# State space scan and SiLU layer on one core: signs of eleven weight blocks on ScalarE, three more W_in blocks in one-pass products, a new order of the ramp

## The chip, the cores and the metric

The kernel runs on one core of one Trainium2 chip. The core has five engines that run side by side and in order, each through its own queue: TensorE (PE, matrix products; PEld is its loading of the stationary operand), VectorE (DVE), ScalarE (ACT), GpSimd (POOL) and SyncE (SP, which here only issues DMA transfers). The metric is the time of one execution on the device, in microseconds (us); lower is better. Before the change the median of three runs is 329.29 us (328.35 to 331.6). A profiled execution of the same kernel was recorded by the hardware profiler, and all views quoted are views of such a record.

## The reference

The first stage is a state space scan (Mamba-2, SSD): for 4 batches and 8 heads over 768 positions, in chunks, with state size 16 and head size 32.

```python
# per batch and head, chunk c, positions i and j in it
cum = cumsum(log(a)); L = exp(cum_i - cum_j) for i >= j
y = (C B^T * L) x + exp(cum_i) * C state          # inside the chunk, and from the state
state = exp(sum log a) * state + sum_j exp(cum_last - cum_j) B_j x_j
```

Its output, turned to 3072 tokens of 256 features, goes through a layer with SiLU, with W_in of 256 x 2048 and W_out of 2048 x 256:

```python
h = x @ w_in
g = h * (1.0 / (1.0 + np.exp(-h)))
return (g @ w_out).astype(np.float32)
```

The weights arrive as 64-bit floats; everything else, and the result, is fp32.

## The kernel before, in words

**Units and groups.** The 3072 tokens are cut into twelve units of 256 tokens (u = 0 to 11, three to a batch), and into six groups of 512 tokens (G = 0 to 5, two units each). For each unit PE does the scan in four bursts of small products: `ab` (decay rows are transposed; units 0 and 1 alone), `g0` (C against B, line 585), `gd` or `D` (B against x, line 571) and `Y` (lines 635 and 644). DVE does the running products `E` (line 512), the masks `M` (line 600) and the state `S` (line 615). ACT moves results out of the accumulators: `X0` (line 666, units 0 and 1) and `y` (line 672), `SM` (line 623), `ce` (line 546), `b` (line 594), `tq` (line 540). For units from 2 on, decays are prepared once for all (`ir` loads, `AA`, `AP`, `AD`), written to a scratch in memory and loaded back (`La`, `Lp`).

**Weight blocks.** W_in is cut into eight blocks of 256 columns (n = 0 to 7) and W_out into eight blocks (n = 8 to 15). A block is loaded raw (`lw,n`, 512 KB, line 288) as pairs of 32-bit words of the 64-bit number, and made into fp32 without arithmetic in 64 bits, over 128 x 512 elements at a time: `u` (ACT, line 294) takes the size of the high word, `v` (ACT, line 297) turns the top bits of the low word into mantissa bits, `w,n,0` and `w,n,1` (DVE, lines 303 and 307) clamp the high word and shift it by three, `w,n,2` (DVE, line 310) puts the sign bit of the high word into v, and `W` (POOL, line 318) adds u and v as integers. Two of the 16 blocks take `W` in two halves.

**Two ways to multiply.** In fp32 a product of 128x512 takes two recorded passes. For most of the work the operands are therefore split into three parts whose products run in one pass each: `H` (ACT, line 322) makes the high part of a weight block, `lD` (DVE, line 326) or `Wl` with `Wm` the low part, `dD` (DVE, line 330) or `Wd` with `We` the third. For the tokens the same three parts are made by `xh` (line 679) and `x,u,0` and `x,u,1` (lines 651 and 654). The first layer is then `a,G,i` (high and low parts, eight products of 128x512 into accumulators ga or gb, line 800), `ax` (ACT, a rescaling in place, line 811), `d` (third part, four products) and `dg` (ACT, SiLU, line 821). The second layer is `q` (line 782) on the parts `h`, `l` and `e` (lines 827, 651 and 837) of the SiLU result.

**Group 0 is done otherwise**, since PE needs work while weights still arrive: W_in blocks 0 to 5 are multiplied in fp32 (`s,u,j`, line 697, for each of the units 0 and 1, into one of three accumulators hp), with `si` (ACT, SiLU, line 703); blocks 6 and 7 go through `a`, `ax`, `d`, `dg`. Its second layer is in fp32: `n1,f,m` (line 761), two accumulators of hp for the whole length.

**What sets the order.** Every instruction stands in a list written out by hand or by a planner beforehand, the string SCHEDULE: its 1309 words are executed from left to right when the program is made, so each engine's queue has its instructions in that order; a second table, SLOTS, says which buffer each tile takes. There is no run-time choice: an engine waits at the head of its queue until the tiles of that instruction are there. The words `z` are products of zeros that keep PE running before it has work (line 441). "The ramp" is here the part up to the point at which the lists of before and after become the same, early in group 1. Loads are issued by SP, except where a word's last number is 1 (ACT's queue) or where POOL issues them (`AD`, `Wm`, `We`).

Of the kernel before, what the change touches and what calls it, by code (L numbers as in the profile page):

```python
# [8 lines left out]
FP32 = mybir.dt.float32  # L9
# [18 lines left out]
Ln,2,0,1,0 xh,1 W,12 x,1,0 w,8,1 v,13 w,13,2 W,13 lw,15 u,15 w,8,2 Ln,2,1,1,0 si,1,5 s,1,4 a,0,7 si,1,4 n1,9,0 H,12  # L28
Wd,12 x,0,1 lw,14 u,14 n1,11,0 n1,9,1 x,1,1 W,8 Ln,2,1,0,0 v,14 w,14,2 ir,0 si,1,0 n1,1,0 n1,1,1 H,0 n1,0,1 H,1 lw,6 v,6
w,6,2 n1,11,1 n1,10,1 ir,2 ir,1 u,6 lw,10 Wl,12 AA,0 AA,1 AD,4 w,6,0 AP w,6,1 AD,0 lw,2 Ln,2,0,0,0 ax,0,7 w,15,0 u,10  # L30
u,2 W,6 n1,8,0 AD,1 v,2 H,6 v,10 w,2,0 s,1,1 si,1,1 lw,3 tp,2 dD,7 v,3 v,15 u,3 w,2,1 w,2,2 W,2,0 Lt,3,1,3,0 lD,6 dD,6
w,14,0 n1,8,1 w,3,2 a,0,6 ax,0,6 w,15,2 W,2,1 s,1,2 si,1,2 H,2 d,0,7 w,14,1 dg,0,7 AD,2 w,3,0 w,15,1 d,0,6 dg,0,6 W,14
Lt,3,1,0,0 w,10,2 s,0,2 lw,9 u,9 v,9 Lt,3,1,2,0 Lt,3,1,1,0 T,3,1 H,4 si,0,2 n1,10,0 Lx,2,0,0 n1,12,1 La,2,0,0 w,3,1 tq,2
# [24 lines left out]
d,2,3 q,2,1,0,0 Lt,7,0,3,0 Vd,1,1 Ln,8,0,0,0 ax,2,2 d,2,2 e,2,0 q,2,0,1,1 q,2,0,0,0 dg,2,3 dg,2,2 Lx,7,0,0 Lt,7,0,1,0
Lt,7,0,2,0 T,7,0 h,2,3 l,2,3 g0,7 gd,7 b,7,0 Lt,8,0,2,0 q,2,0,1,0 q,2,1,1,1 M,7,1 e,2,3 q,2,0,0,1 o,1,0,2 q,2,1,0,1
Lt,8,1,3,0 a,2,5 q,2,3,1,1 Lp,7,0 b,7,1 o,1,1,2 O,1,1,2,2,0 S,7,0 S,7,1 ax,2,5 S,7,2 O,1,0,2,3,0 Lx,8,0,0 M,7,0  # L60
q,2,3,1,0 h,2,2 SM,7,0 S,7,3 O,0,0,2,2,0 La,8,0,0 Lt,8,0,0,0 a,2,4 l,2,2 SM,7,1 ax,2,4 Lt,8,1,0,0 d,2,5 dg,2,5 h,2,5
# [827 lines left out]
```

## Time and profile before

| what | before |
|---|---|
| median of 3 runs | 329.29 us (328.35 to 331.6) |
| the profiled execution: its time, its span | 329.13 us, 327.4 us |
| busy in the span: PE, DVE, ACT, POOL | 319.7, 240.9, 209.6, 55.2 us |
| granted TensorE clock, mean | 0.996 |

The span is from the first to the last recorded instruction; 1.73 us of the execution lie outside it. Busy time is the time in which an engine has at least one instruction under way; matmuls overlap, and their ends are modelled, so a busy PE still may have small holes. The chain view follows the work that ended last back from the end, from each instruction to what released it. A row of the window view gives a stretch's length, and then each engine's busy time in it with the number of instructions. A row of the group view reads: line, engine, operation, tile written and tiles read, shape, count | busy time, mean ns of one | idle time of the engine just before. A row of the timeline reads: start, duration, engine, line, operation, tiles, shape, count, and in brackets the idle time before it with what ended it.

### The profile page before, as it was taken

What the parts mean: (1) busy time and instruction counts of PE and PEld (TensorE: products, weight loads), DVE (VectorE), ACT (ScalarE), POOL (GpSimd) and SP (SyncE); (2) the same over time, 40 slices, a digit from 0 to 9 for tenths busy, and PEclk for the clock granted to TensorE, in tenths of its full rate; (3) what the DMA queues carried; (4) which work ended last, traced back from release to release, by engine and by line L of the source; (5) the groups of instructions that cost most, each with busy time, mean ns of one, the idle gap of its engine ahead of it and who ended that gap; (6) DMA issues with size and microseconds to landing.
All of it is one profiled execution on the core that took longest, in us unless ns stands there. A gap on an engine that the chain in (4) does not pass through costs nothing.

```text
span 327.4 us, 7522 instructions
## 1 busy us (share of the span) xinstructions
PE 319.7 (98%) x3067; PEld 243.1 (74%) x3067; DVE 240.9 (74%) x331; ACT 209.6 (64%) x319; POOL 55.2 (17%) x74
## 2 busy tenths in 40 slices
PE   8889999999999999999999999999999999999994
PEld 4568576655687778878887778878887788888883
DVE  5898999999988966877688199665787544635553
ACT  4679878648696846584761874837775355674641
POOL 1364766316102330000200010010001000000000
PEclk9999999999999999999999999999999999999998
DMA  6999955367872663423632306514042000050002
GB/s 163 208 287 291 271 137 144 52 145 133 149 132 46 104 117 50 90 33 66 143 80 62 51 1 110 110 26 97 3 72 38 9 2 2 0 88 0 2 1 64
DMA packets 94962, 29.27 MB, mean 89 GB/s; under 512 B 80000, under 2 KB 86912, under 8 KB 94928
## 3 DMA queue, kind: packets, MB, share of 16 engines
q1 hardware_dynamic: 90960, 25.71, 36.1%
q0 software_dynamic: 1616, 2.82, 4.9%
q10 hardware_dynamic: 2352, 0.26, 0.6%
q8 instruction: 24, 0.39, 0.5%
q14 instruction: 10, 0.08, 0.1%
HBM read 22.81 MB, written 3.34 MB: 80 GB/s over the span
## 4 chain that ended last, share of the span: by engine, by line
PE 93%; SPq 3%; DMA 2%; issue 0%; DVE 0%; DVEq 0%
PE hp L782 29%; PE ga L800 18%; PE gb L800 18%; PE hp L761 9%; PE hp L697 6%; PE o_ps L782 6%; DMA s2k<-in_B_dram 2%; PE ga L585 2%; PE ga L635 2%; PE ga L644 2%; PE ga L571 1%; PE gb L644 1%; SPq L269 1%; SPq L262 1%; SPq L288 1%; SPq L375 0%
## 5 line engine op out<-in xcount | busy, mean ns | idle before, releaser
L782 PE MATMUL hp<-r4k,s2k 128*128 128x512 f32 x400 | 110.0, 394 | 0.0
L651 DVE SCALAR_TENSOR_TENSOR r4k<-r4k,r4k 128x1024 fp32r<-128x1024 f32 (+1 forms) x42 | 50.4, 1201 | 51.0 <-ACT r4k L827 47.9
L782 PEld LDWEIGHTS hp<-r4k,s2k 128*128 128x128 f32 x400 | 74.0, 188 | 16.4 <-issue 0.3
L800 PE MATMUL ga<-raw,s2k 128*128 128x512 f32 x240 | 62.3, 395 | 0.0
L800 PE MATMUL gb<-raw,s2k 128*128 128x512 f32 x240 | 61.1, 390 | 0.0
L800 PEld LDWEIGHTS ga<-raw,s2k 128*128 128x128 f32 x240 | 44.7, 188 | 11.4 <-ACT ga L811 0.9
L800 PEld LDWEIGHTS gb<-raw,s2k 128*128 128x128 f32 x240 | 44.8, 188 | 9.8 <-ACT gb L811 0.5
L837 DVE SCALAR_TENSOR_TENSOR r4k<-r4k,r4k 128x1024 fp32r<-128x1024 f32 x40 | 49.2, 1231 | 3.4 <-DVE r4k L651 0.9
L827 ACT ACTIVATE r4k<-r4k 128x1024 fp32r<-128x1024 f32 x40 | 42.2, 1058 | 3.2 <-issue 1.3
L811 ACT ACTIVATE ga<-ga 128x1024 f32<-128x1024 f32 x21 | 21.1, 1007 | 24.6 <-PE ga L800 23.8
L811 ACT ACTIVATE gb<-gb 128x1024 f32<-128x1024 f32 x21 | 21.2, 1009 | 17.6 <-PE gb L800 13.3
L782 PE MATMUL o_ps<-r4k,s2k 128*128 128x512 f32 x80 | 30.7, 390 | 0.0
L761 PE MATMUL hp<-r4k,s2k 128*128 128x512 f32 x64 | 30.0, 602 | 0.0
L821 ACT ACTIVATE r4k<-gb 128x1024 f32<-128x1024 f32 x21 | 21.4, 1020 | 12.4 <-PE gb L800 9.9
L520 POOL TENSOR_TENSOR BT<-bn,ab 128x256 f32<-128x256 f32 x10 | 6.7, 671 | 129.2 <-DVE ab L512 129.2
L318 POOL TENSOR_TENSOR s2k<-s2k,s2k 128x512 uint32<-128x512 uint32 (+1 forms) x19 | 23.6, 1249 | 25.8 <-DVE s2k L310 12.7
L821 ACT ACTIVATE r4k<-ga 128x1024 f32<-128x1024 f32 x21 | 21.5, 1023 | 8.4 <-PE ga L800 8.2
L512 DVE TENSOR_TENSOR_SCAN ab<-ab,diag 128x512 f32<-128x512 f32 x20 | 24.8, 1264 | 0.0
L697 PE MATMUL hp<-r4k,s2k 128*128 128x256 f32 x96 | 22.2, 381 | 0.0
L697 PEld LDWEIGHTS hp<-r4k,s2k 128*128 128x128 f32 x96 | 18.0, 190 | 3.9 <-issue 1.4
L761 PEld LDWEIGHTS hp<-r4k,s2k 128*128 128x128 f32 x64 | 11.6, 189 | 10.5 <-issue 9.6
L782 PEld LDWEIGHTS o_ps<-r4k,s2k 128*128 128x128 f32 x80 | 15.0, 188 | 3.2
(123 smaller groups left out, 383.8 us busy)
## 6 DMA issues: line engine op xcount, KB each, us to landing
ab<-az SPq DMA_DIRECT2D x20, 256.0 KB, 4.2
raw<-in_moe_w_in_dram SPq DMA_DIRECT2D x8, 512.0 KB, 4.3
raw<-in_moe_w_out_dram SPq DMA_DIRECT2D x8, 512.0 KB, 6.7
out_dram<-r4k SPq DMA_DIRECT2D x44, 64.0 KB, 2.3
xt<-in_x_dram SPq DMA_DIRECT2D x20, 128.0 KB, 3.6
s2k<-s2k POOLq DMA_DIRECT2D x10, 256.0 KB, 4.0
pfx<-ac SPq DMA_DIRECT2D x10, 130.0 KB
bn<-in_B_dram SPq DMA_DIRECT2D x20, 64.0 KB, 4.6
```

The lines of the kernel that those rows point to most:

```text
L318: nc.gpsimd.tensor_tensor(out=u[:, :, fs], in0=u[:, :, fs], in1=v[:, :, fs], op=ALU.add)
L512: nc.vector.tensor_tensor_scan(out=o, data0=src, data1=diag.rearrange("p h t -> p (h t)"), initial=0.0, op0=ALU.mult, op1=ALU.add)
L644: nc.tensor.matmul(out=y[w][32 * q:32 * q + 32, c, 64 * k:64 * k + 64], lhsT=xc[64 * c:64 * c + 64, k, h], rhs=m[64 * c:64 * c + 64, k, h] ...
L651: nc.vector.scalar_tensor_tensor(out=l, in0=f32(h), scalar=BACK, in1=y, op0=ALU.mult, op1=ALU.add)
L697: nc.tensor.matmul(out=hp[:, i], lhsT=WT[j][:, kc, 128 * i:128 * i + 128], rhs=XM()[:, 2 * kc:2 * kc + 2, u], start=(kc == 0), stop=(kc == ...
L761: nc.tensor.matmul(out=NP[m], lhsT=WT[8 + f // 2][:, f % 2, 128 * m:128 * m + 128], rhs=GT[0, f // 2][:, f % 2], start=(n == 1), stop=(n = ...
L782: nc.tensor.matmul(out=ACC[P, c], lhsT=WK[8 + i, p][:, k, 128 * m:128 * m + 128], rhs={"h": HT, "l": LT, "d": DT}[p][P, i][:, k], start=(n ...
L800: nc.tensor.matmul(out=o, lhsT=WK[j, q][:, kc, 128 * i:128 * i + 128], rhs=xs[:, 2 * kc:2 * kc + 2], start=(start and q == "h" and kc == 0 ...
L811: nc.scalar.activation(t, t, AF.Copy, scale=1.0 + Z)
L821: nc.scalar.activation(g, t, AF.Silu, scale=BACK)
L827: nc.scalar.activation(t, GT[G, i], AF.Copy, scale=-LESS * Z)
L837: nc.vector.scalar_tensor_tensor(out=DT[G, i], in0=f32(HT[G, i]), scalar=-1.0, in1=f32(LT[G, i]), op0=ALU.mult, op1=ALU.subtract)
```

## The change: what it does

1. **Signs on ScalarE.** For blocks 0, 4, 5, 12, 13, 6, 2, 14, 10, 3 and 9 the word `w,n,2` on DVE goes, and a word `g,n` on ACT comes: an activation Sign of the high word, with a bias held in a tile (`above`, a column of one tiny value), that writes +1 or -1 as bf16 into the upper half of each word of v. So that these upper halves are right, `v` is made with half the scale, and all weights come out halved; the five other blocks (7, 1, 8, 11, 15) keep `w,n,2`. The factors of two are given back by scales that instructions have already.
2. **Three more one-pass blocks in group 0.** The six words `s` with their six `si` for blocks 1, 2 and 3 go; `a`, `ax`, `d` and `dg` for G = 0 and i = 1, 2 and 3 come. The parts of the weights that they need were made before too, for the later groups; they now are made earlier.
3. **A new order of the ramp.** The list has 1310 words, and its last 710 are the same as before. The ramp ahead of them is put in another order, loads included, and the table of buffers is new.

```diff
 SCHEDULE
...
-Ln,0,0,0,1 ia,1 ci z,1 z,1 z,1 z,1 z,1 z,1 ia,0 Ln,0,0,1,1 cI z,1 ch cP ct ip,0,0 z,1 z,1 z,1 c1 cd A AT cp AU lw,0 z,1
...
-S,0,3 Ln,1,1,0,0 ab,1,0 E,1,0 C,0 Y,0 X0,0,1 Ln,1,0,1,0 B,1,1 X0,0,0 u,5 w,5,0 ip,1,0 z,1 P01,1,0 tp,1 tq,1 s,0,0 ce,1,1
-ce,1,0 g0,1 Lx,1,1,0 Lx,1,0,0 W,4 xh,0 w,5,1 si,0,0 B,1,0 P01,1,1 D,1 s,0,4 M,1,1 lw,1 u,1 lw,12 S,1,0 W,5 v,1 ca S,1,1
-S,1,2 SM,1,0 SM,1,1 lw,13 s,0,5 si,0,5 v,12 C,1 M,1,0 Y,1 w,1,0 w,1,1 W,7 si,0,4 lw,8 w,1,2 W,1,0 z,1 w,12,2 X0,1,0 H,7
-S,1,3 X0,1,1 x,0,0 lD,7 u,12 w,12,0 w,12,1 u,13 w,13,0 w,13,1 W,1,1 s,0,1 u,8 v,8 s,1,5 ir,3 w,8,0 si,0,1 s,1,0 co
...
+Ln,0,0,0,1 ia,1 ci cA ct z,1 ia,0 z,1 z,1 z,1 cI z,1 lw,0 z,1 z,1 ip,0,0 z,1 Ln,0,0,1,1 z,1 cp z,1 c1 cd Lt,0,1,3,0 z,1 A AT
+AU as,0,0 as,0,1 ch z,1 as,1,0 z,1 ab,0,0 as,1,1 ab,0,1 E,0,1 ab,1,1 lw,4 v,0 E,0,0 z,1 z,1 g,0 z,1 z,1 u,0 Lt,0,1,0,0 w,0,0
+z,1 z,1 Ln,1,0,1,0 cP v,4 P01,0,0 z,1 tp,0 tq,0 g,4 Lt,0,1,1,0 Lt,0,1,2,0 T,0,1 ce,0,1 w,0,1 ab,1,0 Lx,0,0,0 B,0,1 Lx,0,1,0
+W,0,1 lw,7 z,1 E,1,1 z,1 z,1 B,0,0 z,1 Ln,1,0,0,0 z,1 z,1 P01,0,1 u,4 D,0 w,4,0 w,4,1 ce,0,0 g0,0 z,1 z,1 W,4 S,0,0 S,0,1 z,1
+S,0,2 SM,0,0 ir,1 z,1 SM,0,1 M,0,1 M,0,0 C,0 lw,5 S,0,3 z,1 v,7 u,7 z,1 w,7,2 Y,0 Ln,1,1,1,0 z,1 u,5 W,0,0 z,1 v,5 Ln,1,1,0,0
+w,7,0 w,7,1 X0,0,0 tp,1 B,1,1 W,7 X0,0,1 s,0,0 E,1,0 Lx,1,0,0 ca w,5,0 tq,1 ce,1,1 ce,1,0 g0,1 g,5 ip,1,0 si,0,0 H,7 H,0
+P01,1,0 Lx,1,1,0 B,1,0 D,1 lw,1 xh,0 w,5,1 W,5 P01,1,1 s,0,4 v,1 ir,0 S,1,0 S,1,1 ir,2 S,1,2 SM,1,0 si,0,4 u,1 SM,1,1 M,1,1
+M,1,0 lD,7 ir,3 C,1 w,1,2 lw,13 u,13 w,13,0 w,13,1 v,13 s,0,5 si,0,5 Y,1 X0,1,0 AA,0 AD,4 X0,1,1 co lw,12 u,12 AA,1 AP AD,1
+AD,3 v,12 g,12 dD,7 S,1,3 w,12,0 w,12,1 x,0,0 W,12 Ln,2,0,1,0 z,1 z,1 lw,8 g,13 s,1,4 si,1,4 W,13 lw,6 u,8 u,6 w,6,0 xh,1
+lw,2 s,1,5 si,1,5 lw,10 v,6 lw,14 s,1,0 g,6 lw,9 x,0,1 w,6,1 W,6 n1,8,1 v,8 n1,11,1 v,10 Lt,3,1,3,0 n1,11,0 x,1,0 a,0,7
+n1,9,0 w,1,0 si,1,0 w,1,1 W,1,0 Lt,3,1,0,0 lw,3 H,6 u,14 AD,0 n1,9,1 lD,6 a,0,6 AD,2 Lx,3,0,0 w,8,0 w,8,1 Lx,2,1,0 v,2 ax,0,7
+u,10 x,1,1 g,2 u,2 Ln,2,0,0,0 d,0,7 v,14 g,14 w,8,2 W,8 n1,0,1 n1,1,1 n1,1,0 w,2,0 w,14,0 w,14,1 w,2,1 La,2,0,0 dD,6 Lx,2,0,0
+ax,0,6 d,0,6 W,1,1 W,2,0 Ln,2,1,1,0 W,2,1 H,1 lD,1 Lp,2,0 n1,0,0 Ln,2,1,0,0 dg,0,7 tp,2 g,10 W,14 w,10,0 dD,1 v,3 H,2 dg,0,6
+lD,2 dD,2 g,3 La,2,1,0 a,0,1 lw,15 u,15 E,2,0 u,3 n1,13,0 w,10,1 ax,0,1 v,15 E,2,1 ce,2,0 a,0,2 Lt,3,1,2,0 C,2 ax,0,2 w,15,2
+w,15,0 tq,2 d,0,1 La,3,1,0 Lx,3,1,0 n1,12,0 Lt,3,1,1,0 dg,0,1 d,0,2 dg,0,2 w,15,1 W,15 n1,10,0 n1,15,0 n1,13,1 w,3,0 T,3,1
...
-LEAST = 2.0 ** -15
+LEAST = 2.0 ** -15 * 1.25
...
+    above = const.tile([128, 1], FP32, name="above")
...
             if what == "u":
                 u = wu[n] = small(f"u{n}", [128, 2, WF])
                 nc.scalar.activation(u, raw[n][:, :, :, 1].bitcast(FP32), AF.Abs)
+            elif what == "v":
+                v = wv[n] = small(f"v{n}", [128, 2, WF])
+                nc.scalar.activation(v, raw[n][:, :, :, 0], AF.Copy, scale=2.0 ** -52, bias=1.0)
             else:
-                v = wv[n] = small(f"v{n}", [128, 2, WF])
-                nc.scalar.activation(v, raw[n][:, :, :, 0], AF.Copy, scale=2.0 ** -51, bias=2.0)
+                top = wv[n].bitcast(BF16).rearrange("p k (f two) -> p k f two", two=2)[:, :, :, 1]
+                nc.scalar.activation(top, raw[n][:, :, :, 1].bitcast(FP32), AF.Sign, bias=above[:, 0:1])
...
-                             hp.rearrange("p i (c t) -> p i c t", c=2), AF.Silu)
+                             hp.rearrange("p i (c t) -> p i c t", c=2), AF.Silu, scale=2.0)
...
-        nc.scalar.activation(g, t, AF.Silu, scale=BACK)
+        nc.scalar.activation(g, t, AF.Silu, scale=2.0 * BACK)
```

The new function for `cA` fills `above` once (DVE, one memset of 128x1). The weight blocks are loaded in the order 0, 4, 7, 5, 1, 12, 13, 8, 15, 14, 6, 10, 2, 3, 9, 11 before, and in the order 0, 4, 7, 5, 1, 13, 12, 8, 6, 2, 10, 14, 9, 3, 15, 11 after.

More of the change, by code (lines that the diff above doesn't have):

```diff
@@ L29 @@
[L29 to L33, printed above, removed]
@@ L157 @@
     par = const.tile([128, 2], FP32, name="par")
-    const.tile([128, 72], FP32, name="pad")
+    const.tile([128, 64], FP32, name="pad")
     rawp = ctx.enter_context(tc.tile_pool(name="rawp", bufs=7))
@@ L391, in c_tiny, with c_above @@
         nc.scalar.activation(tiny, idle()[:, 0:1], AF.Silu)
+    def c_above():
+        nc.vector.memset(above, 2.0 ** -100)
     def c_ident():
@@ L769, in f_vn @@
     def f_vn(m):
-        nc.scalar.activation(outs(0)[0][:, m], NP[m], AF.Copy)
+        nc.scalar.activation(outs(0)[0][:, m], NP[m], AF.Copy, scale=2.0)
     ACC, NQ = {}, {}
@@ L786, in f_va @@
     def f_va(P, m):
-        nc.scalar.activation(outs(P)[0][:, m], ACC[P, m], AF.Copy, scale=BACK * (1.0 + Z))
+        nc.scalar.activation(outs(P)[0][:, m], ACC[P, m], AF.Copy, scale=2.0 * BACK * (1.0 + Z))
     def f_vd(P, m, half=None):
```

153 lines of the change are left out of this document (72 added, 81 removed), and 6 rows, old and new, of the table SLOTS.

## The prediction

> **What bounds the kernel now.** First the page: busy time by engine, the slices, and the chain of work that ended last.
>
> ```profile
> PE 319.7 (98%) x3067; PEld 243.1 (74%) x3067; DVE 240.9 (74%) x331; ACT 209.6 (64%) x319; POOL 55.2 (17%) x74
> ...
> PE   8889999999999999999999999999999999999994
> ...
> PEclk9999999999999999999999999999999999999998
> ...
> PE 93%; SPq 3%; DMA 2%; issue 0%; DVE 0%; DVEq 0%
> ```
>
> PE is busy from the fourth slice to the last, at full clock, and 93% of the chain is PE; the 5% of SP and DMA must lie before that. The windows tell where, and what the other engines do meanwhile (columns: PE, PEld, DVE, ACT, POOL).
>
> ```profile
> 18.40:45.00 26.60, 26.60 (x255) 19.09 (x254) 24.67 (x40) 21.73 (x41) 16.58 (x20) 1.00 0.93 264
> 45.00:75.00 30.00, 30.00 (x392) 19.51 (x391) 28.36 (x44) 20.38 (x43) 13.68 (x13) 1.00 0.57 126
> 75.00:112.00 37.00, 37.00 (x384) 26.30 (x390) 34.36 (x50) 29.23 (x45) 9.03 (x12) 1.00 0.61 109
> 112.00:322.00 210.00, 210.00 (x1838) 169.58 (x1838) 138.24 (x160) 127.45 (x171) 11.38 (x15) 1.00 0.27 50
> ```
>
> From 18.4 to 322 us PE never rests. In the ramp DVE runs at 93% (87.4 of 93.6 us up to 112) and ACT at 76% (71.3 of 93.6), yet neither holds PE up. So the time is: the start of the dense stream, plus PE's work behind it, plus a tail of 5 us that the change doesn't touch. An edit pays only if it takes work from PE or lets the stream begin sooner; relief of DVE pays nothing by itself. What sets the start is in the chain (start, length, what) and in PE's and SP's timelines.
>
> ```profile
> 11.86 6.14 DMA s2k<-in_B_dram
> 18.59 1.73 PE hp L697 x8
> ```
>
> ```profile
> 16.90 0.27 PE L531 MATMUL o_ps<-ident,s2k 128*128 128x128 f32 x1
> 18.04 0.55 PE L531 MATMUL o_ps<-ident,s2k 128*128 128x128 f32 x3 [0.88 <-DMA s2k<-in_B_dram]
> 18.43 0.81 PE L697 MATMUL hp<-r4k,s2k 128*128 128x256 f32 x3
> ```
>
> The transposes `tp,1` wait for the last of unit 1's loads, issued at 11.86 and landed at 18.0; `s,0,0` stands behind them and starts the stream at 18.43.
>
> **The change part by part: PE's work.** Each of the six words `s` that go is eight records in 1.73 us (above). Each new pair is a word `a` of eight products and a word `d` of four; the same words for group 1 in the chain:
>
> ```profile
> 86.84 1.85 PE ga L800 x8
> ...
> 91.20 0.91 PE ga L800 x4
> ```
>
> 6 x 1.73 = 10.38 us go, 3 x (1.85 + 0.91) = 8.28 come: **-2.1 us**. Since PE is dense, this counts in full. All else on PE (`n1`, `q`, the bursts) has the same count.
>
> **The start.** In the new list `tp,1` still stands ahead of `s,0,0`. Its last load (`Ln,1,1,0`) has the same transfers ahead of it on SP's queue as the load at 11.86 had (x, blocks 7 and 5, B and C of unit 1), and one small load of decays, `ir,1`, besides.
>
> ```profile
> 19.40 0.44 SPq L383 DMA_DIRECT2D s2k<-in_a_dram  x1
> ```
>
> One such issue is 0.44 us; four transposes instead of three follow the landing. I put **+0.2 us**, between -0.9 (the whole wait goes) and +0.6. The scans `E` are earlier for unit 0, but the landing ends last, so that is worth nothing.
>
> **A new wait.** Before, `Y,1` is followed by one `z` and then by `s,0,1`, which needs nothing of it. In the new order two `z` follow and then `s,1,4`, which needs `X0,1,0` and `X0,1,1` on ACT.
>
> ```profile
> 26.37 0.39 PE L441 MATMUL o_ps<-s2k 128*128 128x512 bf16 x1
> 26.60 7.07 PE L697 MATMUL hp<-r4k,s2k 128*128 128x256 f32 x32
> ```
>
> ```profile
> 16.80 0.38 ACT L666 ACTIVATE r4k<-gb 128x256 f32<-128x256 f32 x1
> 17.08 0.38 ACT L666 ACTIVATE r4k<-ga 128x256 f32<-128x256 f32 x1
> ...
> 25.56 0.69 ACT L297 ACTIVATE s2k<-raw 128x512 f32<-128x512 uint32 x1
> ...
> 26.63 0.37 ACT L666 ACTIVATE r4k<-ga 128x256 f32<-128x256 f32 x1
> ```
>
> `X0` began at 26.63; a second one 0.28 behind it ends at 26.63 + 0.28 + 0.38 = 27.29, where PE went on at 26.60: **+0.7 us**, from 0.5 to 1.2. Behind `s,1,4` everything on PE waits.
>
> **ScalarE's load.** Groups of the first 112 us (ns in the second column):
>
> ```profile
> L310 DVE SCALAR_TENSOR_TENSOR s2k<-raw,s2k 128x512 uint32<-128x512 uint32 x16 | 11.7, 739 | 1.5 <-ACT s2k L297 1.3
> L297 ACT ACTIVATE s2k<-raw 128x512 f32<-128x512 uint32 x16 | 10.7, 676 | 3.2 <-DMA raw<-in_moe_w_in_dram 3.2
> L703 ACT ACTIVATE r4k<-hp 128x512 f32<-128x512 f32 x12 | 7.0, 588 | 3.8 <-PE hp L697 3.7
> L821 ACT ACTIVATE r4k<-ga 128x1024 f32<-128x1024 f32 x4 | 4.1, 1026 | 0.4 <-PE ga L800 0.2
> L811 ACT ACTIVATE ga<-ga 128x1024 f32<-128x1024 f32 x4 | 4.0, 1006 | 1.4 <-PE ga L800 1.4
> L546 ACT ACTIVATE ce<-o_ps,par 128x256 f32<-128x256 f32 x4 | 1.7, 487 | 0.0
> L672 ACT ACTIVATE ys<-ga 128x256 f32<-128x256 f32 x3 | 1.1, 382 | 2.0 <-PE ga L644 2.0
> L391 ACT ACT_TABLE_LOAD x1 | 1.3, 1283 | 1.9 <-issue 1.9
> ```
>
> DVE loses 11 x 0.74 = 8.1 us. The trace has no Sign. By the nearest rows it costs what `v` costs, 0.68, plus what an operand read from a tile adds (487 - 382 = 0.11): 0.79. From below it is 0.58 (`v` back to back: the two `X0` above start 0.28 apart though they last 0.38, so neighbours overlap by 0.1). From above: its output is 16 bits wide at every second place, which no row shows; were that written at half speed, 2 x 0.68 + 0.11 = 1.47. I take 0.79, as the row nearest in size. ACT gains 11 x 0.79 = 8.7, and 3 x (1.03 + 1.01 - 2 x 0.59) = 2.6 for part 2: from 71 to 82 us of some 93. That is free as long as ACT isn't late at one place, so I add in the new list's order, at 0.1 less than each duration:
>
> - Up to `Y,1`: from `tq,1` to `SM,1,1` there are 13 activations (`tq`, `ce` twice, `g,5`, `si` twice, `H` twice, `xh`, `v`, `u`, `SM` twice), 7.3 us by durations, 6.0 with the overlap. PE has the same words as before from `s,0,0` to `Y,1`, 6.5 us (18.43 to 24.96, where the row below of that start shows `Y`). Hardly any slack: **+0.2 us**, from 0 to 7.3 - 6.5 = 0.8.
> - Up to `a,0,1`: before, PE took from 18.43 to 46.27 (row below) for its words up to `a,0,6`; the new words up to `a,0,1` are two `s` and one `n1` fewer (0.86, by 7.72 us for 18 records, two each), one `a`, two `d` and one `z` more: 27.8 - 3.5 - 0.9 + 1.9 + 1.8 + 0.2 = 27.3. ACT's 49 words there take 32.7 by durations, 27.8 with the overlap; but the last ones that PE needs at `a,0,1` (`H,1`, `dg,0,7`) come 4 us before the end, and `dg,0,6`, which the next product needs, after 27.1 us of ACT's words, where PE has 29.2. So slack is some 2 us. **0**, at worst 32.7 - 27.3 = 5.4.
>
> ```profile
> 24.96 0.27 PE L635 MATMUL ga<-cw,sm 32*64 32x64 f32 x2
> ```
>
> ```profile
> 35.53 7.72 PE hp L761 x18
> ...
> 46.27 1.86 PE ga L800 x8
> ```
>
> **Moved loads and DVE.** SP's loads are as many bytes. At 264 GB/s (second window) a block takes 2.0 us; block 12 becomes the seventh, so its first word on ACT, at 25.56 before, can run from 27.6, while `n1,8,1` is due at 18.6 + 6.5 + 1.4 + 1.0 + 3 x 1.73 = 32.7. Hidden, by 5 us less the bit words and the addition (some 4). `AP` on DVE and the loads `ir` come before block 12's bits now; if these loads are late, up to 1 us of that is lost. The other sums of DVE fall with its 8 us. I cost these at 0.
>
> **Sum.** -2.1 + 0.2 + 0.7 + 0.2 = -1.0 us. The profiled execution took 329.13 us (span 327.4 and 1.73 around it), 0.16 below the median: **328.1 us**.
>
> **Rivals.**
> - *The start comes forward.* With unit 1's loads partly moved ahead, `tp,1` doesn't wait, and `X0` of unit 0 (done at 17.08 + 0.38) sets the start: -2.1 - 0.9 + 0.7 = 326.8, and where the planned two `z` cover the wait for `X0` as well, 326.1. For it: the load of B at 11.86 is moved to the front. Against: its place at the end of the queue is taken by another 64 KB.
> - *ScalarE becomes the bound (slower).* If `g` is written at half speed, the eight of them up to `a,0,1` cost 8 x 0.68 = 5.4 us more, less the 2 of slack at `dg,0,6`: 3.4 us in which PE waits for `H` and `dg`; 329.13 - 1.2 + 3.4 = **331.3 us**. It turns to slower than before where `g` takes over about 1.2 us, since 8 x 0.4 uses up the slack of 2 and the 1.2 us that the terms before leave. For it: ACT's queue is in order, and takes on 11 us where DVE had 8. Against: up to now no output shape here costs more than its count of elements.
> - *Sign needs another table.* One table load stands in the record, 1.28 us, for Abs, Copy and SiLU together. If Sign needed its own, `g` and `si` or `dg` alternate some seven times in the new order, 13 loads, 17 us on ACT: about 329.1 - 1.2 + 15 = 343 us. The Trainium skill, "ScalarE: Activation LUTs", section "Table sets: the hidden batching unit", says that one set is active at a time and asks to batch by set, and its list of functions found in every set doesn't name Sign; its figure of about 1283 ns for the load agrees with the row.
> - *The clock falls before the stream.* Between `ab` and `D,0` the new order leaves PE fewer `z` in one piece (7 instead of 15), so a hole of some 2.5 us may open. A cold start costs what the first rows show: ten products in 3.72 us, where fifteen warm ones took 3.40 (0.43 and 0.22 each), so 1.5 us: 329.6.
>
> ```profile
> 1.27 3.72 PE L441 MATMUL o_ps<-s2k 128*128 128x512 bf16 x10 [1.27 <-DVE s2k L388]
> ...
> 7.30 3.40 PE L441 MATMUL o_ps<-s2k 128*128 128x512 bf16 x15
> ```
>
> The Trainium skill, "TensorE: Matmul & The Clock Gate", Part 1, states that an idle window of about 3.4 us halves the clock again; the slices here show full clock throughout, so this trace can't test it.
>
> **How the numbers follow.** Forecast 0.62; early start 0.15; ScalarE 0.16; tables 0.02; clock 0.05. A measurement of this kernel tells about 1% (3.3 us) from no change. Faster than 326.0 needs the early start and a little more: 0.12 with the low edge of the forecast. Slower than 332.6 needs the upper part of ScalarE's case or the tables: 0.12. Range: from 325.6 (early start, and no lag anywhere) to 332.2 (ScalarE's case, with +0.6 for the start and +1.2 for `X0`, the upper ends of those terms).
>
> **What would show it.** Line 697 with 48 records instead of 96; line 310 five times; `g` at about 0.8 us; `tp,1` again released by a load near 18 us; a hole of half a microsecond before `s,1,4`; PE dense from there. I am wrong if `g` lasts over 1 us, if PE shows waits on ACT's `H`, `dg` or `ax`, or if the stream starts before 17.8 or after 19.2.

## The result and the profile after

The changed kernel takes 330.41 us (median; 329.39 to 331.45) where the kernel before takes 328.72 beside it: 1.0043 times as long, 95% interval 1.0027 to 1.0059. By that ratio it is 1.4 us slower (1.7 by the medians), where I had forecast some 1 us faster. The profiled execution took 330.84 us (span 328.8), 1.71 more than that of before.

The page of the changed kernel (busy time by engine, PE's slices, granted clock, the chain):

```profile
PE 319.2 (97%) x3055; PEld 240.5 (73%) x3055; DVE 232.1 (71%) x321; ACT 219.8 (67%) x330; POOL 56.6 (17%) x74
...
PE   8899998999999999999999999999999999999994
...
PEclk9999999999999999999999999999999999999999
...
PE 89%; DVE 4%; DMA 3%; ACT 2%; issue 1%; SPq 1%; POOL 0%; DVEq 0%; ACTq 0%; POOLq 0%
```

The work moved as announced: VectorE has ten instructions fewer in all, ScalarE eleven more, and PE twelve records fewer. But PE's busy time fell by only 0.5 us in a span that is 1.4 longer: PE now rests. The chain says so too; it runs over DVE, DMA and ACT for 9%. The windows show where (columns: PE, PEld, DVE, ACT, POOL, clock, DMA share, GB/s):

```profile
18.40:45.00 26.60, 26.60 (x256) 19.14 (x255) 23.86 (x41) 26.21 (x49) 17.89 (x22) 1.00 0.91 256
45.00:75.00 30.00, 28.82 (x378) 16.61 (x377) 23.20 (x38) 24.97 (x47) 10.69 (x11) 1.00 0.56 128
75.00:112.00 37.00, 36.34 (x343) 25.96 (x343) 30.38 (x42) 28.09 (x45) 9.01 (x11) 1.00 0.43 83
112.00:322.00 210.00, 210.00 (x1868) 169.54 (x1867) 140.12 (x164) 128.51 (x171) 12.47 (x16) 1.00 0.29 56
```

Before, PE was busy for the whole of the second and third stretch; now it rests 1.8 us there. The view of waits gives PE's own between 45 and 90 us (us in total, times, longest); the same view of before has no row at all:

```profile
PE gb L803 <- ACT gb L814: 0.6, 1, 0.6
PE ga L638 <- ACT sm L626: 0.5, 2, 0.3
PE hp L764 <- POOL s2k L318: 0.4, 1, 0.4
PE ga L588 <- ACT r4k L824: 0.3, 1, 0.3
```

By name: `d,0,1` waits for `ax,0,1`; `Y,3` and `Y,4` for `SM`; `n1,15,0` for block 15's addition `W`; `g0,4` for `dg,1,0`. Ends of matmuls are modelled, so a wait is larger than its row. Measured from start to start of neighbouring words, less the usual distance, they are 0.73 us before `d,0,1`, 0.52 before `n1,15,0`, 0.23 before `Y,2`, 0.36 before `Y,3`, 0.48 before `g0,4` and 0.51 before `Y,4`: 2.8 us. With the start of the stream 0.58 us later (19.01 in place of 18.43), 0.31 more outside the span, PE's words 2.1 less and one `z` more (0.2), that makes 1.8; 1.71 were measured. From the first word on PE that both lists share (`q,1,3,1,1`, at 112.70 before and at 114.20 now) to the last product of `q`, the one takes 209.7 us and the other 209.5. All of the loss lies in the ramp.

Two of the waits have one origin. The timelines of SP, ACT and POOL in the changed kernel show it:

```profile
38.71 0.60 SPq L251 DMA_DIRECT2D tbc<-in_C_dram  x1
42.03 0.61 SPq L234 DMA_DIRECT2D pfx<-ac  x1
...
43.96 0.55 SPq L285 DMA_DIRECT2D raw<-in_moe_w_out_dram  x1
```

```profile
49.38 1.23 ACT L291 ACTIVATE s2k<-raw 128x512 f32<-128x512 f32 x2 [1.63 <-DMA raw<-in_moe_w_out_dram]
```

```profile
54.38 1.39 POOL L318 TENSOR_TENSOR s2k<-s2k,s2k 128x512 uint32<-128x512 uint32 x1 [7.55 <-DMA tbc<-in_B_dram]
```

SP is held at `Lp,2,0` until 42.03, since it needs the decays that are still being written, so block 15's load leaves at 43.96. ACT then stands 1.63 us at `u,15`, with `ax,0,1` queued behind, and `W,15` ends only at 55.8. (The bracket at `W,15` names a load of other data; what it needs is block 15's own words, and the last of them, `w,15,1`, ended on VectorE at 54.30.) In the order before, SP came to that load at 20.5 (timeline of SP before):

```profile
20.51 2.08 SPq L288 DMA_DIRECT2D raw<-in_moe_w_out_dram  x1
```

### The profile page after: what moved, and what is told of

The parts are those of the page before. It is cut to its first block, busy times and chain, and to the rows that moved or that the text cites. A ratio compares the mean times of both kernels' runs of the same rounds, so it can differ in the third digit from the quotient of the medians.

```text
span 328.8 us, 7484 instructions
## 1 busy us (share of the span) xinstructions
PE 319.2 (97%) x3055; PEld 240.5 (73%) x3055; DVE 232.1 (71%) x321; ACT 219.8 (67%) x330; POOL 56.6 (17%) x74
## 4 chain that ended last, share of the span: by engine, by line
PE 89%; DVE 4%; DMA 3%; ACT 2%; issue 1%; SPq 1%; POOL 0%; DVEq 0%; ACTq 0%; POOLq 0%
PE hp L785 29%; PE gb L803 18%; PE ga L803 17%; PE o_ps L785 6%; PE hp L764 5%; PE hp L700 3%; PE o_ps L444 2%; PE ga L638 2%; PE ga L588 2%; PE ga L647 2%; DMA raw<-in_moe_w_out_dram 2%; PE gb L647 1%; DVE ab L515 1%; DMA tbc<-in_B_dram 1%; PE ga L574 1%; ACT sm L626 1%
## 5 line engine op out<-in xcount | busy, mean ns | idle before, releaser
L654 DVE SCALAR_TENSOR_TENSOR r4k<-r4k,r4k 128x1024 fp32r<-128x1024 f32 (+1 forms) x42 | 50.5, 1202 | 51.4 <-ACT r4k L830 50.6
L785 PEld LDWEIGHTS hp<-r4k,s2k 128*128 128x128 f32 x400 | 74.0, 188 | 16.3 <-issue 0.3
L814 ACT ACTIVATE ga<-ga 128x1024 f32<-128x1024 f32 x22 | 22.2, 1008 | 23.8 <-PE ga L803 23.1
L814 ACT ACTIVATE gb<-gb 128x1024 f32<-128x1024 f32 x23 | 23.2, 1009 | 16.2 <-PE gb L803 12.0
L824 ACT ACTIVATE r4k<-gb 128x1024 f32<-128x1024 f32 x23 | 23.4, 1020 | 13.4 <-PE gb L803 10.6
L824 ACT ACTIVATE r4k<-ga 128x1024 f32<-128x1024 f32 x22 | 22.5, 1021 | 9.8 <-PE ga L803 9.6
L515 DVE TENSOR_TENSOR_SCAN ab<-ab,diag 128x512 f32<-128x512 f32 x20 | 23.9, 1205 | 0.0
L764 PEld LDWEIGHTS hp<-r4k,s2k 128*128 128x128 f32 x64 | 11.5, 189 | 9.4 <-issue 6.5
L554 POOL TENSOR_TENSOR cw<-ct,pfx 128x256 f32<-128x256 f32 x9 | 8.8, 983 | 32.7 <-DMA pfx<-ac 14.2
L603 DVE TENSOR_TENSOR ab<-gb,ab 128x512 f32<-128x512 f32 x12 | 8.3, 688 | 8.0 <-PE gb L588 8.0
```

What stands on the lines that cost most here:

```text
L515: nc.vector.tensor_tensor_scan(out=o, data0=src, data1=diag.rearrange("p h t -> p (h t)"), initial=0.0, op0=ALU.mult, op1=ALU.add)
L654: nc.vector.scalar_tensor_tensor(out=l, in0=f32(h), scalar=BACK, in1=y, op0=ALU.mult, op1=ALU.add)
L764: nc.tensor.matmul(out=NP[m], lhsT=WT[8 + f // 2][:, f % 2, 128 * m:128 * m + 128], rhs=GT[0, f // 2][:, f % 2], start=(n == 1), stop=(n = ...
L785: nc.tensor.matmul(out=ACC[P, c], lhsT=WK[8 + i, p][:, k, 128 * m:128 * m + 128], rhs={"h": HT, "l": LT, "d": DT}[p][P, i][:, k], start=(n ...
L814: nc.scalar.activation(t, t, AF.Copy, scale=1.0 + Z)
L824: nc.scalar.activation(g, t, AF.Silu, scale=2.0 * BACK)
```

## The experiments

Ratios are against the kernel before, run beside each of them; the intervals are 95%.

**1. Which engine do the signs load?** Three kernels: the signs back on VectorE in the new order, the signs alone in the old order, and no signs in the new order. A fourth leaves them out in the old one.

```diff
 e3_dve:    the new order, each g,n -> w,n,2 (11 times)
 e4_signs:  the order and buffers of before, each of the eleven w,n,2 -> g,n
 e5_nog:    the new order, the eleven g,n left out
 e8_nosign: e4_signs with the eleven g,n left out
```

> The changed kernel with all eleven signs back on VectorE at the same places (`w,n,2` for `g,n`). If the signs overload ScalarE: 9.4 us leave it, PE's waits on `ax`, `SM`, `X0` and `dg` before 75 us go, and 1.5 to 3 us come off: 327.4 to 328.9. If order and missing fillers are the cause: VectorE gains 8.1 us where it was 93% busy, so PE waits at least as much: 330.4 to 333.

> The order of the kernel before, with the eleven `w,n,2` turned into `g,n` (and halved weights), nothing else of the change. If the signs overload ScalarE: PE waits on ScalarE in the first 112 us, and the time is 330 or more where the kernel before takes 328.7. If order and missing fillers are the cause: the same as before, 328.4 to 329.0, as PE's words are the same and in the same order.

> The changed kernel without its eleven `g` (the signs of eleven weight blocks are left out, by nobody made up for): 9.4 us of work less on ScalarE, none more anywhere, order as it is. If ScalarE's load is what makes PE wait in the new order: the waits before `d,0,1`, `Y,2`, `Y,3`, `g0,4`, `Y,4` (2.2 us) shrink by more than half and the time is 327.4 to 328.9. If the order (start, late block 15) and the missing fillers are the cause: the same waits stay, at most 0.3 us each less, 329.8 to 330.4.

> The order of the kernel before without the signs of the eleven blocks (left out, on neither engine; the other five as before): 8.1 us less on VectorE than the kernel before, and 9.4 us less on ScalarE than with `g` in this order (331.9). If PE alone bounds the kernel before, as the forecast took it, relief of VectorE is worth nothing: 328.4 to 329.0. The price of the signs on ScalarE in this order is then the 3 us between the two. If VectorE holds PE up in places: 326.5 to 328.

| kernel | us | ratio |
|---|---|---|
| e3_dve | 336.56 | 1.0234 (1.0213 to 1.0256) |
| e4_signs | 331.92 | 1.0088 (1.0066 to 1.0110) |
| e5_nog | 330.44 | 1.0040 (1.0024 to 1.0055) |
| e8_nosign | 328.65 | 0.9995 (0.9979 to 1.0011) |

In the new order the signs on ScalarE cost nothing that shows: without them the ratio is the same (1.0040 and 1.0043; together the two intervals leave some 0.7 us open). In the old order they cost 1.0088 - 0.9995, or 3.1 us. There VectorE stands idle behind ScalarE's late `u`, and PE then waits for an addition on POOL (timelines of DVE and of PE in e4_signs):

```profile
41.83 0.43 DVE L299 TENSOR_SCALAR s2k<-s2k 128x512 f32<-128x512 f32 x1 [4.48 <-ACT s2k L287]
```

```profile
50.86 1.35 PE L696 MATMUL hp<-r4k,s2k 128*128 128x256 f32 x5 [1.68 <-POOL s2k L314]
```

So the new order makes room for the signs; what it pays for that has to lie elsewhere. And relief of VectorE by 8.1 us in the old order is worth nothing that shows (0.9995, 0.9979 to 1.0011), as forecast; the reverse in the new order (e3_dve) costs 6 us, part of it a fall of the clock (last section).

**2. The start and the late block.** What stands ahead of the first product of real data in the changed kernel (timeline of PE):

```profile
1.27 4.87 PE L444 MATMUL o_ps<-s2k 128*128 128x512 bf16 x11 [1.27 <-DVE s2k L388]
6.08 0.31 PE L456 MATMUL o_ps<-ident,s2k 32*128 32x32 f32 x1
```

Eleven cold `z` stand ahead of `AT`, whose operand was there at 4.7 us.

```diff
 e1_z:     -z z z z A AT ... ab,1,1          +A AT ... ab,1,1 z z z z
 e2_lw15:  -lw,3 ... a,0,1 lw,15             +lw,3 lw,15 ... a,0,1
 e6_both:  both
```

> The changed kernel with four of the eleven `z` that stand ahead of `AT` on PE put behind `ab,1,1` instead. If the cold `z` set the start (order theory): `AT` at 5.0 instead of 6.08 us, the first scan `E` near 7.2 instead of 8.26, `s,0,0` at 18.0 to 18.4 instead of 19.01, and 0.6 to 1.0 us off the time: 329.4 to 329.8. If the start hangs on VectorE's or GpSimd's order behind the scans and not on `AT`: `AT` earlier but `s,0,0` still at 19.0, and the time 330.4. The theories on ScalarE and on missing fillers expect 330.4 as well, less what the start gives.

> The changed kernel with the load of block 15 issued right behind that of block 3. If that late load makes PE wait (order theory): the waits of PE before `d,0,1` (0.73 us) and before `n1,15,0` (0.52 us) go, ScalarE's 1.63 us of idle time before `u,15` goes, and 0.8 to 1.3 us come off: 329.1 to 329.6. If ScalarE is full with the eleven signs anyway: `ax,0,1` is as late as before, PE waits the same 0.7 us behind other words of ScalarE, time 330.2 to 330.5. If missing fillers are the cause: these two waits may go, but the ones at `Y,2`, `Y,3`, `g0,4` and `Y,4` (1.6 us) stay.

> The changed kernel with both edits: four `z` behind `ab,1,1` and block 15's load behind block 3's. Order theory: the start comes 1.0 us forward, `X0` on ScalarE takes that back before `s,1,4` (0.99 us of wait, as with the four `z` alone), and block 15's waits go: 329.2 to 330.0. If ScalarE's queue isn't what holds `X0`, the wait before `s,1,4` is under 0.3 us and the time 328.2 to 329.2.

e1_z took 331.17 (1.0064, 1.0044 to 1.0083), e2_lw15 329.98 (1.0037, 1.0021 to 1.0054), e6_both 330.21 (1.0025, 1.0008 to 1.0041). In e1_z `AT` comes at 4.53 and the stream starts at 17.95, as hoped, and nothing is gained: ACT's queue stands at block 13's load, with `X0,1` behind it (timeline of ACT in e1_z).

```profile
25.21 0.69 ACT L291 ACTIVATE s2k<-raw 128x512 f32<-128x512 f32 x1 [0.94 <-DMA raw<-in_moe_w_out_dram]
...
26.87 0.36 ACT L669 ACTIVATE r4k<-ga 128x256 f32<-128x256 f32 x1
27.13 0.37 ACT L669 ACTIVATE r4k<-gb 128x256 f32<-128x256 f32 x1
```

PE waits 0.99 us there (start to start; 0.82 in the view). In e2_lw15 the waits before `d,0,1` and `n1,15,0` are gone from the record; of the 1.25 us that they made up, the ratios show 0.2 (1.0043 and 1.0037) and the medians 0.4, all within the intervals. Single executions of one of these kernels lie up to 3 us apart, and a wait in one profile isn't the median's: before `s,1,4` the changed kernel's profile has no wait, and that of e12_pad (below), with the same ramp, has 0.47 us.

**3. Do the waits go, or move?** On top of e6_both the words of blocks 13 and 1 are put behind those that PE needs; three `n1` are moved to the bursts where PE waits; then both.

```diff
 e9_ahead (on e6_both):
-v,1 ... u,1 SM,1,1 ... u,13 w,13,0 w,13,1 v,13 s,0,5 si,0,5 Y,1 X0,1,0 AA,0 AD,4 X0,1,1
+SM,1,1 v,1 u,1 ... s,0,5 si,0,5 Y,1 X0,1,0 AA,0 AD,4 X0,1,1 u,13 w,13,0 w,13,1 v,13
 e10_fill (on the changed kernel):
-n1,10,0 n1,15,0 n1,13,1 ... g0,2 ... n1,14,0 n1,4,0 g0,3
+n1,15,0 ... g0,2 ... n1,4,0 g0,3 gd,3 n1,12,1 n1,13,1 ... n1,6,0 n1,14,0 ... n1,4,1 n1,10,0 ... Y,4
 e11_all: both
```

> The changed kernel with the four `z` behind `ab,1,1`, block 15's load behind block 3's, and on ScalarE the words of blocks 13 and 1 that wait for late loads put behind the words PE needs (`u,13`, `v,13` and the bit words behind `X0,1,1`; `v,1`, `u,1` behind `SM,1,1`). If PE waits because ScalarE's queue, in order, stands at the head of a block that hasn't landed: the waits before `Y,1` (0.45 us in one profile), `s,1,4` (0.99 in another) and `d,0,1` go, the start stays at 18.0, and the time is 328.4 to 329.2, with a narrower spread of its runs. If these waits only move to the next block's words: 329.8 to 330.4, as with the two edits alone.

> The changed kernel with three words `n1` moved later, as fillers: `n1,13,1` behind `n1,12,1` (ahead of `Y,3`), `n1,14,0` behind `n1,6,0` (ahead of `g0,4`), `n1,10,0` behind `n1,4,1` (ahead of `Y,4`). Same work on every engine. If missing fillers in the scan bursts make PE wait: the waits of 0.36, 0.48 and 0.51 us there go, and 0.8 to 1.3 us come off: 329.1 to 329.6. If the other engines' words are late in any case: PE waits as long at `g0,2`, `g0,3` or the places named, 330.2 to 330.7.

> The edits of the two kernels above together. If late loads in front of ScalarE's words and missing fillers are two causes apart: both gains add, 327.2 to 328.4, under the kernel before. If the one takes the place of the other: 328.6 to 329.6.

e9_ahead 331.28 (1.0048, 1.0020 to 1.0076), e10_fill 331.07 (1.0048, 1.0020 to 1.0075), e11_all 331.49 (1.0060, 1.0034 to 1.0086): no gain. The views of PE's waits say why. In e9_ahead nothing waits at `Y,1` or `s,1,4` any more, but the blocks that were put back are now late themselves (18 to 45 us):

```profile
PE hp L762 <- POOL s2k L316: 0.8, 2, 0.5
```

In e10_fill the waits at `Y,3`, `g0,4` and `Y,4` are gone, so they were for want of something to do; PE came to `n1,15,0` and to unit 3 sooner and waited there instead (17 to 112 us, two of the three rows):

```profile
PE hp L765 <- POOL s2k L319: 1.2, 1, 1.2
...
PE ga L575 <- POOL BT L524: 0.4, 1, 0.4
```

**4. What are the one-pass products worth?** The six `s` put back, in the new order, as fillers in the bursts.

```diff
 e7_s3:
-a,0,1 ... ax,0,1 a,0,2 ... ax,0,2 d,0,1 n1,12,0 dg,0,1 d,0,2 dg,0,2
+s,0,1 ... si,0,1 s,0,2 ... si,0,2 n1,12,0 s,1,1 si,1,1
-gd,2 n1,5,1 n1,5,0 n1,14,1 Y,2 n1,15,1 a,0,3 ax,0,3 ... d,0,3 dg,0,3
+gd,2 n1,14,1 s,1,2 n1,15,1 si,1,2 Y,2 n1,5,1 n1,5,0 ... s,0,3 si,0,3
-gd,3 n1,12,1 n1,3,0 Y,3 ... gd,4 n1,3,1 n1,4,1 Y,4
+gd,3 n1,12,1 s,1,3 si,1,3 Y,3 ... gd,4 n1,3,1 n1,4,1 n1,3,0 Y,4
 e13_s3b (on e7_s3): si,0,1 right behind s,0,1, and lw,15 right behind lw,3
```

> The changed kernel with the one-pass products of blocks 1, 2 and 3 turned back into six `s`, put as fillers where PE waits (`s,1,2` ahead of `Y,2`, `s,1,3` ahead of `Y,3`, one `n1` more ahead of `Y,4`); signs and all else of the order stay. PE has 2.1 us more to do, ScalarE 2.6 us less. If the missing fillers cost the 2.1 us: the waits before `d,0,1`, `Y,2`, `Y,3` and `Y,4` (1.8 us) go, so the time is 330.2 to 330.9, about what the changed kernel takes: that part is worth nothing net. If fillers don't matter: the waits stay and 2.1 us come on top, 332 to 332.6. If ScalarE's load is the cause: the 2.6 us off it pay too, 329.0 to 329.9.

> The kernel with six `s` in place of the one-pass products of blocks 1 to 3, mended: `si,0,1` right behind `s,0,1` on ScalarE (not behind block 15's words), and block 15's load behind block 3's. The first version took 333.6 with 1.8 us of wait at this `si`. If the one-pass products gain their 2.1 us of PE in full: 332.1 to 332.6, 2.1 over the changed kernel with block 15's load early (330.0). If the waits in the scan bursts eat the gain: 329.8 to 331.0.

e7_s3 took 333.58 (1.0138, 1.0111 to 1.0164), with a wait of my own making: `si,0,1` stood behind block 15's words. e13_s3b, without it, took 331.22 (1.0075, 1.0048 to 1.0102). Against e2_lw15 (1.0037), which differs from it in the products, the places of six words `n1` between them and the buffers, that is 0.38% or 1.2 us: what the one-pass products gain net, of 2.1 us that they take off PE. By the two intervals it is 0.2 to 2.2 us. In e13_s3b PE's waits between 45 and 90 us are

```profile
PE ga L588 <- ACT r4k L824: 0.3, 1, 0.3
PE hp L764 <- POOL s2k L318: 0.3, 1, 0.3
```

so those at `Y` are gone. I read it so: a word `s` needs only an accumulator of hp and can stand between the bursts as filler, where `a` and `d` need ga and gb, the very accumulators of the bursts. That is argued from these two rows, not shown: e10_fill gave the bursts fillers of another kind and gained nothing. The other side is that even without the one-pass products the new order is 2.4 us slower than the old (1.6 to 3.4).

**5. Is work on PE worth its time at all?** Words of `d` left out, so that PE alone has less to do.

```diff
 e14_bd67:   the kernel before    -d,0,7 -d,0,6
 e15_ad67:   the changed kernel   -d,0,7 -d,0,6
 e16_ad123:  the changed kernel   -d,0,1 -d,0,2 -d,0,3
 e17_relief: e16_ad123, without the eleven g,n, with lw,15 right behind lw,3
 e18_bns67:  e14_bd67, without the eleven signs
```

> The kernel before without `d,0,6` and `d,0,7` (the third products of blocks 6 and 7 for the first 512 tokens are left out): 8 records, 1.8 us less on PE, near 50 us, nothing else changed. If PE alone paces the kernel before (the step of the forecast: PE is dense, so its words count in full): 1.8 us off, 326.8 to 327.3. If the other engines and the loads stand right behind PE there and set the pace as soon as it is faster: 0 to 0.7 us off, 328.1 to 328.9.

> The changed kernel without the same two words. If PE paces the new order at that place: 1.8 us off, 328.4 to 328.9. If the others do: 329.7 to 330.6, and the waits of PE at `a,0,2`, `d,0,1`, `n1,15,0` grow by what was taken out.

> The changed kernel without `d,0,1`, `d,0,2` and `d,0,3` (the third products of blocks 1 to 3 left out): 2.7 us less on PE between 50 and 70 us. If PE paces it: 327.6 to 328.2. If the others do: 329.6 to 330.6, with PE's waits longer at `g0,2`, `g0,3` and in the bursts behind them.

> The changed kernel without its eleven signs and without `d,0,1` to `d,0,3` (both left out), and with block 15's load behind block 3's: 9.4 us less on ScalarE and 2.7 us less on PE, and the late block mended. If PE and ScalarE together pace the new order, or block 15 alone stood in the way: 326.8 to 328.0. If the chain through VectorE and GpSimd (bits, additions, scans) or the loads pace it: 329.0 to 330.0, as with the load alone (330.0).

> The order of the kernel before without the signs of the eleven blocks and without `d,0,6`, `d,0,7` (both left out): 8.1 us less on VectorE and 1.8 us less on PE than the kernel before. Without the signs alone it took 328.65, without the two words alone 328.19. If PE and VectorE stand side by side and each hides the other: 326.8 to 327.4. If the loads and GpSimd pace it: 327.9 to 328.6.

| kernel | less on PE | us | ratio | to compare with |
|---|---|---|---|---|
| e14_bd67 | 1.8 us | 328.19 | 0.9985 (0.9962 to 1.0009) | 1 |
| e15_ad67 | 1.8 | 330.10 | 1.0028 (1.0011 to 1.0045) | 1.0043 |
| e16_ad123 | 2.7 | 331.00 | 1.0053 (1.0027 to 1.0078) | 1.0043 |
| e17_relief | 2.7, ScalarE 9.4 | 329.20 | 1.0016 (1.0002 to 1.0029) | 1.0037 |
| e18_bns67 | 1.8, VectorE 8.1 | 327.83 | 0.9973 (0.9962 to 0.9985) | 0.9995 |

This is the answer. Taken from PE alone, 1.8 us are worth 0.5 us in either order (0.9985 and 1.0043 - 1.0028, times 329; the intervals allow nothing and allow 1.2, but not 1.8). With VectorE relieved as well (e18_bns67 against e8_nosign) they are worth 0.7, and 2.7 us with ScalarE relieved as well (e17_relief against e2_lw15) also 0.7. In e16_ad123 the 2.7 us show no gain at all, but its executions fall apart by the clock: the six with a mean granted clock of 0.997 or more have a median of 329.7 us, 0.7 under the changed kernel, and the five with 0.994 or less took 331.8 to 332.2. In the profile, which is one of these five, a fall of the clock takes 1.6 us back (last section).

What comes up behind PE differs by place. In the kernel before, the two words stood between `s,1,2` and `s,0,2`. The second of these can't begin before `si` has emptied the accumulator of the first, since two of the three in hp belong to `n1` by then (timeline of PE in e14_bd67):

```profile
48.71 1.89 PE L694 MATMUL hp<-r4k,s2k 128*128 128x256 f32 x8
51.29 1.99 PE L694 MATMUL hp<-r4k,s2k 128*128 128x256 f32 x8 [0.69 <-ACT r4k L700]
```

From start to start that is 2.58 us where a word `s` takes 1.73: 0.85 of the 1.8 us come back at once (e18_bns67 has the same wait of 0.69). So in the old order the two words also covered a hand-over of PE's own work, and their test says less about other places. In the new order it is another chain. In e17_relief, where the load and ScalarE are out of the way, VectorE is busy for 10.93 of the 11 us from 42.5 to 53.5 (in the kernel before, 10.97 there; in the changed kernel, whose ACT waits for the load, 9.78):

```profile
42.50:53.50 11.00, 9.67 (x36) 5.96 (x35) 10.93 (x16) 8.73 (x14) 4.75 (x5) 1.00 0.82 175
```

At its end stands the last bit word of block 15, then `W,15`, then PE (timelines of DVE, POOL and PE in e17_relief):

```profile
51.45 0.43 DVE L307 TENSOR_SCALAR s2k<-s2k 128x512 uint32<-128x512 uint32 x1
```

```profile
51.95 1.38 POOL L318 TENSOR_TENSOR s2k<-s2k,s2k 128x512 uint32<-128x512 uint32 x1 [6.25 <-DMA pfx<-ac]
```

```profile
53.39 1.98 PE L764 MATMUL hp<-r4k,s2k 128*128 128x512 f32 x4 [1.33 <-POOL s2k L318]
```

And a part of what VectorE does there came with the change: up to 56 us it makes the low and third parts of four blocks now, since `a,0,1` and `a,0,2` need them, where the old order made three low and two third ones (groups of DVE from 18.4 to 56 us, before and then after):

```profile
L326 DVE TENSOR_TENSOR s2k<-s2k,s2k 128x512 fp32r<-128x512 f32 x3 | 2.0, 673 | 0.0
L330 DVE SCALAR_TENSOR_TENSOR s2k<-s2k,s2k 128x512 fp32r<-128x512 f32 x2 | 1.8, 894 | 0.0
```

```profile
L330 DVE SCALAR_TENSOR_TENSOR s2k<-s2k,s2k 128x512 fp32r<-128x512 f32 x4 | 3.8, 952 | 0.0
L326 DVE TENSOR_TENSOR s2k<-s2k,s2k 128x512 fp32r<-128x512 f32 x4 | 3.3, 818 | 0.0
```

That is 3.3 us more of the 8.1 that the signs had freed, at the place where it counts.

**6. The time outside the span.** It is 1.73 us before and 2.07 after (medians); e12_pad adds eleven small writes on VectorE behind `q,2,0,1,1`.

> The changed kernel with eleven writes of 128x1 (of a tile that nobody reads) added on VectorE behind the middle of the run, where it has free time. The time outside the span is 1.73 us in the kernel before and 2.07 in the changed kernel, in all its runs; the one variant of its order with VectorE's count as before had 1.71. If that 0.34 us hangs on VectorE's number of instructions: 1.7 outside, time 330.0 to 330.2. If not: 2.07 outside, 330.4.

Outside are now 1.73 us (median), and the time is 330.43 (1.0028, 1.0006 to 1.0050), the same as without them (330.41) within the intervals. The number of VectorE's instructions alone isn't what decides: e4_signs and e8_nosign have 321, as the changed kernel has, and 1.75 and 1.71 us outside in the old order; e10_fill and e11_all, with 321 in nearly the new order, have 1.96 and 1.85. What sets these 0.34 us, and whether they cost anything, stays open.

No kernel that does the whole computation beat the one before; of the changed ones e6_both came nearest. Eight results lie by 0.2 us or more above every range that I had written down for them (e1_z, e3_dve, e6_both, e7_s3, e9_ahead, e10_fill, e11_all, e16_ad123).

## Why the prediction was wrong

**The step that failed** is the first sum: "6 x 1.73 = 10.38 us go, 3 x (1.85 + 0.91) = 8.28 come: -2.1 us. Since PE is dense, this counts in full." The words are as long as I took them; the conclusion isn't so. A dense PE shows that nothing else was later than PE, not by how much. 1.8 us less on PE gave 0.5 in the kernel before itself (e14_bd67, at most 1.2 by its interval) and 0.5 in the changed one (e15_ad67). Of the 2.1 us, 1.2 came through (e13_s3b against e2_lw15, 0.2 to 2.2). That is 0.9 of the 2.4 us between the forecast and the measurement; the other 1.5 belong to the new order, which I had at +1.1 in all (start, `X0`, ScalarE) and which by these two ratios and the changed kernel's costs some 2.6, each of these figures good to about 1 us.

**The second failed step** is "Moved loads and DVE", costed at 0. I checked one block, number 12; block 15 went from ninth to fifteenth place in the loads, behind an issue that SP had to wait with, and 1.25 us of PE's waits in the profile hang on it. I counted VectorE's 8 us of relief and not the parts of blocks 1 and 2 that move ahead of block 15's bits. And I counted the slack of ScalarE at two words only, where in order queues make every late load a wait for whatever stands behind it. Without the one-pass products, and with block 15's load mended, the new order is still 2.4 us slower than the old (e13_s3b); its single waits can't be added up, since those that were removed were followed by others elsewhere (e1_z, e9_ahead, e10_fill). Which share each of loads, VectorE and GpSimd has in these 2.4 us stays open.

**The start**, +0.2 forecast: 0.58 measured, and not for my reason. `tp,1` no longer waits for a load; the cold `z` ahead of `AT`, and the scans behind it, set it. But e1_z starts the stream 1 us sooner and isn't faster.

**The wait for `X0`**, +0.7: none; the two `z` cover it in this profile (+0.2 for one `z` more). It is 0.47 in e12_pad, and 0.99 with the earlier start of e1_z.

**ScalarE**, +0.2: 0. The groups of the changed kernel up to 112 us:

```profile
L700 PE MATMUL hp<-r4k,s2k 128*128 128x256 f32 x48 | 11.0, 383 | 0.0
...
L297 ACT ACTIVATE s2k<-raw,above 128x512 bf16<-128x512 f32 x11 | 9.5, 874 | 0.1
...
L310 DVE SCALAR_TENSOR_TENSOR s2k<-raw,s2k 128x512 uint32<-128x512 uint32 x5 | 3.9, 775 | 0.0
```

A Sign takes 0.87 us where I had put 0.79, and 0.80 back to back; it is under the 1.2 from which I saw trouble, and e5_nog shows no cost. Of my signs of being wrong one came: PE waits for `ax,0,1` and for `dg,1,0`. A long Sign isn't the reason: block 15's load stands behind the first, and the row of the second is the same in e5_nog, without any of the eleven.

**The rivals.** "ScalarE becomes the bound" came out near in time (331.3) and is wrong in cause: leaving the signs out changes nothing. That 330.41 us lies inside my range, whose upper end is this rival's, is therefore luck. (Its lower end, 325.6, doesn't follow from my terms, which give 326.1.) The rival is right for the old order (3.1 us), which I didn't weigh. "The start comes forward" didn't happen; e1_z brings it about, without the gain. "Sign needs another table" is out: one table load stands in the record of the changed kernel as before, so there Sign, Abs, Copy and SiLU came out of one set. "The clock falls" didn't happen in the changed kernel; it did in the profiles of e3_dve and e16_ad123.

## What to carry to other kernels

That an engine is busy all the time doesn't make its work worth its duration: look how late the next engine would be, and measure it by leaving a few of its words out, at more than one place, before spending anything on making them cheaper. In queues that run in order, a load that lands late delays whatever stands behind its first reader, so a new order has to be gone through load by load; one block as an example isn't enough. A word that PE does between two others may also cover a hand-over between them (the words `d` between two `s`), so making it cheaper or taking it out can open a hole.

## What the runs showed of the hardware

**In two profiles the clock fell after a hole of little over 2 us, and stayed down for 3.4.** In e16_ad123 PE stood 2.40 us, and the clock was at half from about 55.0 to 58.4; the timeline of PE and the windows around it:

```profile
51.02 1.88 PE L764 MATMUL hp<-r4k,s2k 128*128 128x512 f32 x4
55.30 3.52 PE L764 MATMUL hp<-r4k,s2k 128*128 128x512 f32 x4 [2.40 <-POOL s2k L318]
```

```profile
54.00:55.00 1.00, 0.00 (x0) 0.00 (x0) 1.00 (x3) 1.00 (x3) 1.00 (x1) 1.00 0.05 11
55.00:56.00 1.00, 0.70 (x1) 0.50 (x2) 0.53 (x1) 1.00 (x3) 1.00 (x3) 0.51 0.18 43
56.00:57.00 1.00, 1.00 (x2) 0.34 (x1) 0.00 (x0) 0.92 (x2) 1.00 (x2) 0.50 0.14 41
57.00:58.00 1.00, 1.00 (x2) 0.34 (x1) 0.00 (x0) 0.00 (x0) 1.00 (x2) 0.50 0.00 0
58.00:59.00 1.00, 1.00 (x18) 0.25 (x24) 0.00 (x0) 0.00 (x0) 0.48 (x1) 0.79 0.00 0
```

The same four products took 1.88 us before the hole and 3.52 behind it, 1.6 us on top of the wait. In e3_dve a hole of 2.13 us, up to 46.81, was followed by half clock from 48 to about 51.4 (windows):

```profile
48.00:50.00 2.00, 2.00 (x3) 0.68 (x2) 2.00 (x4) 1.76 (x3) 1.68 (x2) 0.50 1.06 343
50.00:52.00 2.00, 2.00 (x6) 1.19 (x5) 2.00 (x2) 0.63 (x1) 2.00 (x2) 0.65 1.23 197
```

A hole of 1.68 us in e4_signs left the clock at full. The Trainium skill, "TensorE: Matmul & The Clock Gate", Part 1, gives a free-running window of 3413 ns and the fall after one idle window. The slow stretches here agree with that length; the holes were shorter than it, so PE need not be idle for a whole window's length.

**VectorE's words stretch beside GpSimd's additions.** In the changed kernel POOL added from 43.22 to 46.82; the same word on DVE took 1.22 us within it and 0.68 behind it (timelines of POOL and of DVE):

```profile
43.22 3.60 POOL L318 TENSOR_TENSOR s2k<-s2k,s2k 128x256 uint32<-128x256 uint32 x3 [1.24 <-DVE s2k L307]
```

```profile
43.59 1.22 DVE L326 TENSOR_TENSOR s2k<-s2k,s2k 128x512 fp32r<-128x512 f32 x1
...
47.30 0.68 DVE L326 TENSOR_TENSOR s2k<-s2k,s2k 128x512 fp32r<-128x512 f32 x1
```

The others that ran there do the same: line 303 took 0.96 us at 44.73 and 0.42 at 53.42, line 330 took 1.77 at 45.61 and 0.69 at 48.02. That is a reading of one trace, in which spans on POOL are rough; no run takes the additions away. So a mean of a group on VectorE, such as the 0.74 us that I used for `w,n,2`, may hold some of GpSimd's time too.
